# One scale per batch for the queries of the last two batches of a block-sparse attention with a rational feed-forward

## The chip, the cores and the metric

The kernel runs on one core of a Trainium2 chip. The time is that of the device in microseconds, the median of three runs. The core has five instruction streams that run side by side, each in order: PE (TensorE, the matmuls), DVE (VectorE), ACT (ScalarE), POOL (GpSimd), and SP (SyncE), which here issues the DMA transfers. They wait for each other by semaphores.

## The reference

Four batches (B = 4) of 8 heads, 768 positions and 64 features go through a block-sparse attention (blocks of 32; each block sees its neighbours, the first and the last block, and three sampled ones), and the 3072 x 512 result goes through a feed-forward whose middle is a quotient of polynomials:

```python
scores = scale * np.matmul(q, k.transpose(0, 1, 3, 2))
...
attn = np.exp(scores)
attn = attn / (np.sum(attn, axis=-1, keepdims=True) + 1e-09)
return np.matmul(attn, v).astype(np.float32)
...
h = x @ w_in
P = a[0] + a[1] * h + a[2] * h2 + a[3] * h3
Q = 1.0 + np.abs(b[0]) * np.abs(h) + np.abs(b[1]) * h2
g = P / (Q + 1e-06)
return (g @ w_out).astype(np.float32)
```

## The kernel before

The program first makes a list of pieces of work (`Op`: engine, price, what must be done before, which buffers it takes, a due number `prio`), and `issue` then puts them in one fixed order per engine, by a model of the prices. A change of a few pieces therefore moves others too. At run time every engine works through its list in order and waits where a list says so.

Queries and keys are split into two float16 parts, high and low, after they were multiplied by a power of two. That scale comes from a bound on the largest entry: ACT sums absolute values (`bound`, L392), PE turns the 128 sums onto one partition's row (L343, a 128 x 128 transpose), DVE takes their maximum (L348) and makes the scale in four small instructions (L351 to L360).

For keys and values there is one such scale a batch (`prep`): six loads `ld` of 128 x 512 (L588), six bounds, one scale, and for keys a second round of loads (L540) that are split, turned on PE (L668) and stored. All of these loads, and the staging of the output, take buffers of one ring (`r_ld`, three, and four more once the weights are decoded).

For queries there is one scale for each tile of four blocks (`prep_q`, six tiles a batch, 24 in all): SP loads `ldq` (L711), ACT bounds it (L392), PE turns the sums (L343), DVE makes the scale and the factor of the scores `cq` (L729 to L735), POOL makes the high part (L154), DVE the low part (L386), PE turns both (L741), ACT takes them from PSUM (L745), and SP swaps halves (L749). `ldq` has one buffer, which is free again after the low part.

Around it run the attention of one block after the other (scores L884, maxima L894 and L923 on DVE, exponentials L912 on ACT, transposes L953, values L1010, and for four blocks together the normalisation L1044 and the transposes L1056) and the feed-forward in units: 24 matmuls `into` (L1121 to L1123), squares and the like on ACT (L1128 to L1152), the quotient on DVE (L1135 to L1166, ending with the high part `gh`, L1156, and the low part `gl`, L1166), and 12 matmuls `out` (L1177 with `gh`, L1178 with `gh`, L1179 with `gl`, four times).

In what follows the batches are called first to fourth (b = 0 to 3 in the code), and the query tiles of a batch first to sixth.

Of the kernel before, what the change touches and what calls it, by code (L numbers as in the profile page):

```python
# [23 lines left out]
def kernel(  # L24
# [117 lines left out]
    def among(key, home, **prices):  # L142

        d = {{"ve": VE, "sc": SC, "po": PO}[n]: p for n, p in prices.items()}
        return {home: d[home], **(d if key in ALT else {})}
# [395 lines left out]
                          in_=src[b, g * HU:(g + 1) * HU, t * CH:(t + 1) * CH].rearrange("h (p s) d -> p h (s d)", s=2))  # L541

    PLAIN = B
    s_kall = [Slot(r_kg) for _ in kgs]

    def prep(b, when):
# [7 lines left out]
        before = {}  # L554
        if first:
            rings = [[(r_tt, "tt", p2), (r_ab, "ab", p2), (r_sq, "sq", p2)], [(r_pr, "pr", p3), (r_ld, "ld", p3)]]
        for w in range(2):
            mx, lds, los = {}, {}, []

            def mx_tile(mx=mx):  # L560
                if 0 not in mx:
                    mx[0] = p4.tile([P, 8], F32, name="mx")
                return mx[0]

            for j in range(n):
                def one(j, w=w, lds=lds, mx_tile=mx_tile):
# [11 lines left out]
                    def load():  # L578
                        if first:
                            nb = {"tt": 3, "pr": 4}.get(tag)  # L580
                            d["ld"] = pool.tile([P, 512], F32, name=tag, bufs=nb)
                            if w:
                                nc.sync.dma_start(out=d["ld"], in_=v[b].rearrange("h (a r) d -> (h a) (r d)", a=P // H)[:, j * 512:(j + 1) * 512])
                            else:
                                load_unit(k, b, *units[j], d["ld"])
                        else:
                            d["ld"] = new_ld(slot)
                            nc.sync.dma_start(out=d["ld"], in_=(k, v)[w][b].rearrange("h (a r) d -> (h a) (r d)", a=P // H)[:, j * 512:(j + 1) * 512])  # L588

                    def most():  # L590
                        bound(d["ld"], mx_tile()[:, j:j + 1])
# [6 lines left out]
            def out_scale(s, inv):  # L598
                kv[b][4] = p4.tile([P, 1], F32, name="xscale", bufs=B)
                nc.vector.tensor_copy(out=kv[b][4], in_=s)  # L600

            def largest(mx=mx, w=w):
                nc.vector.tensor_reduce(out=mx[0][:, 6:7], in_=mx[0][:, 0:n], axis=AX.X, op=ALU.max)
# [94 lines left out]
    def prep_q(b, t, prio, before):  # L698
# [1 line left out]


        d = qt[b, t] = {}
        s_ld, s_hl, s_sc, s_ps = Slot(r_ldq), Slot(r_hlq), Slot(r_scq), Slot(r_sp)
        d["slot"], d["cslot"] = Slot(r_qa), Slot(r_cq)

        def load():
            d["ld"] = p1.tile([P, 512], F32, name="ldq")
# [16 lines left out]
            split16(d["ld"], sc[0], d["hl"], 0, None)  # L724

        def factor():
            d["cc"] = p4.tile([P, 2], F32, name="cq")
            d["c"], d["cn"] = d["cc"][:, 0:1], d["cc"][:, 1:2]
            nc.vector.scalar_tensor_tensor(out=d["c"], in0=sc[1], scalar=SCALE, in1=kv[b][2], op0=ALU.mult, op1=ALU.mult)  # L729

# [20 lines left out]
            d["q"] = [x.rearrange("p (h g) r -> p g h r", g=2) for x in (qa, qc)]  # L751

        o_ld = Op(SY, [(650, 262144 // 2 // len(runs(t)))] * 2 * len(runs(t)), load, (), prio - 1, takes=[s_ld], behind=before)
        o = Op(SC, 613, most, [o_ld], prio, uses=[s_ld])
        o, sc = scales(lambda: d["mx"][:, 0:1], "scq", [o], prio, [s_sc])
        h = Op(among("q", PO, po=671, ve=396, sc=613), 0, high, [o], prio, takes=[s_hl], uses=[s_ld, s_sc])
        l = Op(VE, 663, low, [h], prio, uses=[s_ld, s_hl, s_sc])
        d["oc"] = row(VE, [(70, factor), (69, factor2), (69, factor3)], [o, k_scale[b]], prio, takes=[d["cslot"]], uses=[s_sc])
        x = Op(TE, 445, transposes, [l], prio, takes=[s_ps], uses=[s_hl])
        x = Op(SC, 904, evac, [x], prio, takes=[d["slot"]], uses=[s_ps])  # L760
        d["oq"] = Op(SY, [(650, 131072)] * 2, swap, [x], prio, uses=[d["slot"]])
# [42 lines left out]
    def attention(b, j, prio):  # L804
# [15 lines left out]
        for m, x in enumerate(xs):  # L820
            def one(m, x):
# [84 lines left out]
                def exps():  # L906
                    st = d["st"]
                    for g in range(2):
                        if "sm" not in G:
                            G["sm"] = p4.tile([P, 3, 2 * XB], F32, name="sm", bufs=2)  # L910
                        total = G["sm"][:, 0, 2 * e4 + g:2 * e4 + g + 1]
                        nc.scalar.activation(out=prs[x][:, g], in_=prs[x][:, g], func=AF.Exp, scale=Q["c"], bias=st[:, 6 + g:7 + g],  # L912
                                             accum_out=total if n == 1 else st[:, 8 + 2 * m + g:9 + 2 * m + g])

                return s_pr, exps
# [4 lines left out]
            return 71, lambda: nc.vector.tensor_tensor(out=d["st"][:, 0:2], in0=d["st"][:, 0:2], in1=d["st"][:, 2 * e:2 * e + 2], op=ALU.max)  # L920

        def negative():
            nc.vector.tensor_scalar(out=d["st"][:, 6:8], in0=d["st"][:, 0:2], scalar1=Q["cn"], scalar2=PS_EXP * math.log(2.0), op0=ALU.mult, op1=ALU.add)  # L923

        omax = row(VE, [larger(e) for e in range(1, n)] + [(130, negative)], omax, prio[-1], uses=[s_st, Q["cslot"]])
        for m, x in enumerate(xs):
            s_pr, exps = d[m]
            oexp.append(Op(SC, 1172, exps, [omax], prio[m] + 0.1, takes=[G["s_sm"]] if e4 == 0 and m == 0 else [],
                           uses=[s_pr, s_st, Q["cslot"]] + ([] if e4 == 0 and m == 0 else [G["s_sm"]])))

        def total(e):
            def run():
# [324 lines left out]
    def when(b):  # L1257
        if b == 0:
            return lambda w, stage, j: (-83.96, -78.19)[w] + stage * 0.5
        p0 = part_prio(first_of[b])  # L1260
        A = [8.9, 8.52] if b == 1 else [11.69, 8.81]
        return lambda w, stage, j: p0 - A[stage] + (w * 6 + j) * (([0.5, 0.5] if b == 1 else [0.85, 0.83])[stage])

    prep(0, when(0))
    chain["edges"] = Op(PO, 1400, edges, [o for t in range(NCH) for o in k_evac[0, t]], -40, uses=s_kall)
# [61 lines left out]
```

## Time and profile before

| | |
|---|---|
| median of three runs | 891.03 us (888.12 to 893.66) |
| the profiled execution | 892.74 us, of it 890.9 us from the first to the last instruction |
| PE busy with matmuls | 833.8 us, 94% |
| DVE, ACT, POOL busy | 737.1 us (83%), 676.7 us (76%), 109.9 us (12%) |
| mean granted TensorE clock | 0.973 of full speed |
| chain that ended last | 65% PE, 9% DMA, 9% DVE, 7% ACT, 6% SP's issuing |
| moved by DMA | 148.01 MB, 166 GB/s |

Busy time counts instructions of the engine itself, not waits. The first 290 us hold the decoding of the weights and much waiting; after that PE has a matmul in flight nearly all the time.

### The profile page before, as it was taken

The page shows a single profiled execution, that of the slowest core. Times are in us where ns is not written, and L with a number is a line of the kernel's source. Part 1 is how long each engine was busy: PE and PEld are TensorE (multiplying, and loading weights), DVE is VectorE, ACT ScalarE, POOL GpSimd, SP SyncE. Part 2 cuts the span into 40 slices and gives each one's busy share as a digit, 9 for nine tenths or more (in the row PEclk, how much of TensorE's full clock was granted, in tenths as well). Part 3 has the DMA queues.
Part 4 walks back from the last instruction along what each step waited for, and adds up shares of the span by engine and source line. Part 5 has one row for each costly group of instructions (what it writes and reads, how often), then busy time and mean ns, then how long its engine had stood idle before and what let it go on. Part 6 is the DMA issues. An engine that isn't in the chain of part 4 may idle for free.

```text
span 890.9 us, 27280 instructions
## 1 busy us (share of the span) xinstructions
PE 833.8 (94%) x10349; PEld 646.3 (73%) x10349; DVE 737.1 (83%) x1826; ACT 676.7 (76%) x1451; POOL 109.9 (12%) x114
## 2 busy tenths in 40 slices
PE   8988686897899999899999999999999999999997
PEld 4454464675678787688877787778888777788885
DVE  5657998899999888689877978779888887788885
ACT  6777897897687878598767887898768678767563
POOL 1113631616310000100000000100000000000000
PEclk9999798798999999899999999999999999999999
DMA  7798589778856965699756965698567566640000
GB/s 201 186 169 197 169 180 207 209 199 226 177 152 160 261 184 150 149 230 230 160 147 168 277 176 148 166 235 223 152 152 179 153 172 157 165 108 24 1 24 24
DMA packets 238481, 148.01 MB, mean 166 GB/s; under 512 B 16016, under 2 KB 222736, under 8 KB 238352
## 3 DMA queue, kind: packets, MB, share of 16 engines
q1 hardware_dynamic: 238352, 146.29, 65.6%
q8 instruction: 82, 1.34, 0.7%
q14 instruction: 47, 0.39, 0.2%
HBM read 128.92 MB, written 11.01 MB: 157 GB/s over the span
## 4 chain that ended last, share of the span: by engine, by line
PE 65%; DMA 9%; DVE 9%; ACT 7%; SPq 6%; issue 3%; ACTq 0%; POOL 0%; DVEq 0%; POOLq 0%
PE acc L1177 9%; PE acc L1178 8%; PE acc L1179 8%; PE ph L1121 8%; PE ph L1122 7%; PE ph L1123 7%; PE av L1010 5%; PE sp L884 4%; PE pt L953 4%; DMA vg<-in_v_dram 3%; DMA ldq<-in_q_dram 2%; ACT pr L912 1%; ACT scrap L392 1%; DMA wl<-in_moe_w_out_dram 1%; SPq L980 1%
## 5 line engine op out<-in xcount | busy, mean ns | idle before, releaser
L1121 PE MATMUL ph<-xh,wi 128*128 128x256 f16 x768 | 213.1, 278 | 0.0
L1122 PE MATMUL ph<-xl,wi 128*128 128x256 f16 x768 | 211.9, 276 | 0.0
L1123 PE MATMUL ph<-xh,wi 128*128 128x256 f16 x768 | 211.7, 276 | 0.0
L912 ACT ACTIVATE pr<-pr,st,cq 128x256 f32<-128x256 f32 x224 | 132.2, 593 | 46.4 <-DVE st L923 46.2
L1177 PE MATMUL acc<-wo_h,gh 128*128 128x512 f32 x384 | 165.4, 431 | 0.2 <-ACT ld L150 0.2
L1179 PE MATMUL acc<-wo_h,gl 128*128 128x512 f32 x384 | 154.5, 402 | 3.5 <-DVE gl L1166 3.5
L1178 PE MATMUL acc<-wo_l,gh 128*128 128x512 f32 x384 | 153.9, 401 | 0.8 <-POOL wo_l L459 0.8
L1145 DVE SCALAR_TENSOR_TENSOR ab<-sq,absb,ab 128x512 f32<-128x512 f32 x96 | 73.7, 768 | 46.4 <-ACT ab L1142 46.3
L1128 ACT ACTIVATE sq<-ph,fc 128x512 f32<-128x512 f32 x96 | 65.5, 682 | 57.3 <-PE ph L1123 56.9
L1121 PEld LDWEIGHTS <-wi 128*128 128x128 f16 x768 | 76.2, 99 | 28.7 <-issue 15.8
L894 DVE CUSTOM_DVE_ANT_1 pr<-sp,bias 128x256 f32<-128x256 f32 x224 | 84.7, 417 | 9.4 <-PE sp L884 9.3
L1179 PEld LDWEIGHTS acc<-wo_h,gl 128*128 128x128 f32 x384 | 73.5, 191 | 22.4 <-DVE gl L1166 4.8
L1177 PEld LDWEIGHTS acc<-wo_h,gh 128*128 128x128 f32 x384 | 74.0, 193 | 17.0 <-issue 2.3
L1156 DVE SCALAR_TENSOR_TENSOR gh<-tt,par,rr 128x512 fp32r<-128x512 f32 x96 | 72.7, 757 | 14.0 <-PE acc L1178 13.4
L1178 PEld LDWEIGHTS acc<-wo_l,gh 128*128 128x128 f32 x384 | 73.9, 193 | 13.5 <-POOL wo_l L459 1.7
L154 POOL TENSOR_SCALAR hlq<-ldq,scq 128x512 f16<-128x512 f32 x24 | 21.4, 892 | 504.9 <-DVE scq L360 306.6
L1123 PEld LDWEIGHTS <-wi 128*128 128x128 f16 x768 | 76.1, 99 | 9.6
L953 PE MATMUL pt<-ident,pr 128*128 128x128 f32 x448 | 76.8, 293 | 6.1 <-ACT pT L150 4.6
L1010 PE MATMUL av<-vg,pT 128*32 128x64 f32 x3584 | 74.2, 224 | 8.8 <-DMA vg<-in_v_dram 4.8
L1122 PEld LDWEIGHTS <-wi 128*128 128x128 f16 x768 | 76.2, 99 | 8.0
L953 PEld LDWEIGHTS pt<-ident,pr 128*128 128x128 f32 x448 | 68.0, 206 | 18.3 <-ACT pT L150 6.2
L1010 PEld LDWEIGHTS av<-vg,pT 128*32 128x32 f32 x3584 | 56.4, 111 | 33.9 <-issue 10.9
(144 smaller groups left out, 1651.5 us busy)
## 6 DMA issues: line engine op xcount, KB each, us to landing
vg<-in_v_dram SPq DMA_DIRECT2D x312, 64.0 KB, 3.3
vg<-in_v_dram SPq DMA_DIRECT2D x88, 192.0 KB, 3.9
vg<-in_v_dram SPq DMA_DIRECT2D x24, 512.0 KB, 5.4
kall<-ks SPq DMA_DIRECT2D x49, 192.0 KB, 3.7
kall<-ks SPq DMA_DIRECT2D x147, 64.0 KB, 2.1
ld<-in_k_dram SPq DMA_DIRECT2D x36, 256.0 KB, 5.6
wl<-in_moe_w_in_dram SPq DMA_DIRECT2D x32, 256.0 KB, 4.8
wl<-in_moe_w_out_dram SPq DMA_DIRECT2D x16, 512.0 KB, 4.6
```

The source lines that it names most:

```text
L894: nc.vector.tensor_tensor_reduce(out=prs[x][:, g].rearrange("p (s r) -> p s r", r=BLK), in0=h["sp"][:, g].rearrange("p (s r) -> p s r", r= ...
L912: nc.scalar.activation(out=prs[x][:, g], in_=prs[x][:, g], func=AF.Exp, scale=Q["c"], bias=st[:, 6 + g:7 + g], accum_out=total if n == 1 e ...
L953: nc.tensor.transpose(pp[:, jj * P:(jj + 1) * P], cols, ident)
L1010: nc.tensor.matmul(av[rows, g], pT[:, 2 * g + kt, rows] if plain else pT[:, 2 * g + kt, pa_, rows], vf[:, g * HG + h4, kt * D:(kt + 1) * D ...
L1121: nc.tensor.matmul(o, wh, xh[:, :, cc], start=(cc == 0), stop=False)
L1122: nc.tensor.matmul(o, wh, xl[:, :, cc], start=False, stop=False)
L1123: nc.tensor.matmul(o, wl, xh[:, :, cc], start=False, stop=(cc == NCC - 1))
L1145: nc.vector.scalar_tensor_tensor(out=d["ab"], in0=d["sq"], scalar=absb[:, 1:2], in1=d["ab"], op0=ALU.mult, op1=ALU.add)
L1156: nc.vector.scalar_tensor_tensor(out=d["gh"], in0=d["tt"], scalar=par[:, 0:1], in1=d["rr"], op0=ALU.add, op1=ALU.mult)
L1177: nc.tensor.matmul(acc[:, t], ghs, wo_h[:, f], start=(new and e == 0), stop=False)
L1178: nc.tensor.matmul(acc[:, t], ghs, wo_l[:, f], start=False, stop=False)
L1179: nc.tensor.matmul(acc[:, t], gls, wo_h[:, f], start=False, stop=(last and e == 1))
```

## The change

For the third and the fourth batch (`QB = 2`) `prep` runs a pass more, `w == 2`, ahead of those of keys and values: six loads `ld` of the whole batch of queries, six bounds on ACT, one maximum on DVE, one transpose on PE and one scale. The six tiles of such a batch have no bound, transpose and scale of their own any more: the high part waits for the load `ldq` and for the batch's scale alone. Their factor `cq` is made once a batch. The first two batches are as before.

```diff
+    QB = 2
+    q_scale = {}
...
-        for w in range(2):
+        for w in ([2] if b >= QB else []) + [0, 1]:
...
-                            nc.sync.dma_start(out=d["ld"], in_=(k, v)[w][b].rearrange("h (a r) d -> (h a) (r d)", a=P // H)[:, j * 512:(j + 1) * 512])
+                            nc.sync.dma_start(out=d["ld"], in_=(k, v, q)[w][b].rearrange("h (a r) d -> (h a) (r d)", a=P // H)[:, j * 512:(j + 1) * 512])
...
+            if w == 2:
+                def largest(mx=mx):
+                    nc.vector.tensor_reduce(out=mx[0][:, 6:7], in_=mx[0][:, 0:n], axis=AX.X, op=ALU.max)
+
+                o = Op(VE, 75, largest, los, when(w, 0, n - 1))
+                q_scale[b] = scales(lambda mx=mx: mx[0][:, 6:7], "scqb", [o], when(w, 0, n - 1))
+                continue
...
-        o = Op(SC, 613, most, [o_ld], prio, uses=[s_ld])
-        o, sc = scales(lambda: d["mx"][:, 0:1], "scq", [o], prio, [s_sc])
-        h = Op(among("q", PO, po=671, ve=396, sc=613), 0, high, [o], prio, takes=[s_hl], uses=[s_ld, s_sc])
-        l = Op(VE, 663, low, [h], prio, uses=[s_ld, s_hl, s_sc])
-        d["oc"] = row(VE, [(70, factor), (69, factor2), (69, factor3)], [o, k_scale[b]], prio, takes=[d["cslot"]], uses=[s_sc])
+        if own:
+            o = Op(SC, 613, most, [o_ld], prio, uses=[s_ld])
+            o, sc = scales(lambda: d["mx"][:, 0:1], "scq", [o], prio, sl_sc)
+        else:
+            o, sc = q_scale[b]
+        h = Op(among("q", PO, po=671, ve=396, sc=613), 0, high, [o, o_ld], prio, takes=[s_hl], uses=[s_ld] + sl_sc)
+        l = Op(VE, 663, low, [h], prio, uses=[s_ld, s_hl] + sl_sc)
+        if own or t == 0:
+            d["oc"] = row(VE, [(70, factor), (69, factor2), (69, factor3)], [o, k_scale[b]], prio, takes=d["cslot"], uses=sl_sc)
+            d["first"] = d
+        else:
+            d["first"], d["oc"] = qt[b, 0], qt[b, 0]["oc"]
...
-        return lambda w, stage, j: p0 - A[stage] + (w * 6 + j) * (([0.5, 0.5] if b == 1 else [0.85, 0.83])[stage])
+        return lambda w, stage, j: p0 - A[stage] + ((w * 6 if w < 2 else -3) + j) * (([0.5, 0.5] if b == 1 else [0.85, 0.83])[stage])
```

In the changed kernel PE, DVE, ACT and POOL keep their order up to the place of 290 us in the trace of before; PE's list is the same up to 342.7 us and again from 797.5 us on. Line numbers behind the first edit are higher by 2 to 19 (L1166 is L1185, L923 is L942, L711 is L723, L588 is L590). Three places of the new order matter here, all at the sixth query tile of the third batch.

DVE, where the quotient of a unit ends with `gl`. Before:

```order
L1162 SCALAR_TENSOR_TENSOR tt<-tt,par,ab 128x512
L1044 TENSOR_TENSOR xn<-av,sm 128x512
L1166 TENSOR_TENSOR gl<-tt,rr 128x512
L348 TENSOR_REDUCE scq<-sp 128x1
L351 TENSOR_SCALAR scq<-scq 128x1
```

Now:

```order
L1181 SCALAR_TENSOR_TENSOR tt<-tt,par,ab 128x512
L1063 TENSOR_TENSOR xn<-av,sm 128x512
L386 SCALAR_TENSOR_TENSOR hlq<-ldq,scqb,hlq 128x8x64
L942 TENSOR_SCALAR st<-st,cqb 128x2
L1185 TENSOR_TENSOR gl<-tt,rr 128x512
```

The low part of the query tile (L386) has moved up by eight places and now stands ahead of `gl`; the negative maxima (L923, now L942), which stood ahead of L1162, stand behind it too.

SP, the loads ahead of that tile's `ldq` (the ISA rows prepare an address that was read at run time). Before:

```order
L856 DMA kall<-ks 128x256
L711 DMA ldq<-in_q_dram 64x4x128 x2
L974 DMA vg_111<-in_v_dram 48x8x128
L980 ISA
L980 DMA vg_111<-in_v_dram 16x8x128
```

Now:

```order
L875 DMA kall<-ks 128x256
L590 DMA ld<-in_k_dram 128x512
L723 DMA ldq<-in_q_dram 64x4x128 x2
L993 DMA vg_111<-in_v_dram 48x8x128
L999 ISA
```

A load of keys of the fourth batch, the fifth of six for its bound, stands just ahead of `ldq`; the fourth of them stands ten DMAs further up, ahead of a group `vg`, and the sixth behind the next group `kall`. In the trace of before all six were issued between 484.3 and 497.0 us, ahead of the fifth query tile's load.

PE, behind the 24 matmuls `into` of the same unit. Before:

```order
L343 MATMUL sp<-ident,mxq 128x128
L1177 MATMUL acc<-wo_h,gh 128x512
L1178 MATMUL acc<-wo_l,gh 128x512
L1179 MATMUL acc<-wo_h,gl 128x512
```

Now:

```order
L1075 MATMUL sp<-ident,xn 128x128 x4
L1196 MATMUL acc<-wo_h,gh 128x512
L1197 MATMUL acc<-wo_l,gh 128x512
L1198 MATMUL acc<-wo_h,gl 128x512
```

The transpose of the tile's own bound is gone, the four transposes L1056 (now L1075) have taken its place, and the `out` matmuls follow at once; the transposes of the tile itself (L741, now L753) follow the twelve `out` matmuls.

## Rows read from the trace of the kernel before

**Rows 1.** The page, section 1: busy us (share of the span) and instructions.
```profile
PE 833.8 (94%) x10349; PEld 646.3 (73%) x10349; DVE 737.1 (83%) x1826; ACT 676.7 (76%) x1451; POOL 109.9 (12%) x114
```

**Rows 2.** Busy times by stretch: length, engines, granted clock, DMA share, GB/s.
```profile
550.00:575.00 25.00, 22.77 (x253) 18.29 (x251) 19.32 (x47) 17.34 (x33) 3.60 (x4) 0.93 0.62 164
600.00:625.00 25.00, 25.00 (x342) 20.72 (x338) 23.12 (x71) 21.86 (x49) 0.69 (x1) 1.00 0.83 226
```

**Rows 3.** Waits of the whole run: total us, times, longest us.
```profile
ACT scrap L392 <- DMA ldq<-in_q_dram: 20.4, 8, 5.9
```

**Rows 4.** PE's timeline, sixth query tile, second batch: start, length, what, idle before.
```profile
359.10 0.27 PE L1123 MATMUL ph<-xh,wi 128*128 128x256 f16 x1
362.73 0.48 PE L343 MATMUL sp<-ident,mxq 128*128 128x128 f32 x1 [3.36 <-ACT scrap L392]
...
369.45 0.27 PE L1121 MATMUL ph<-xh,wi 128*128 128x256 f16 x1
```

**Rows 5.** PE's timeline at the sixth query tile of the third batch.
```profile
556.60 0.27 PE L1123 MATMUL ph<-xh,wi 128*128 128x256 f16 x1
559.10 0.32 PE L343 MATMUL sp<-ident,mxq 128*128 128x128 f32 x1 [2.23 <-ACT scrap L392]
...
564.54 0.27 PE L343 MATMUL sp<-ident,mx 128*128 128x128 f32 x1
564.65 0.27 PE L1121 MATMUL ph<-xh,wi 128*128 128x256 f16 x1
```

**Rows 6.** PE's timeline: the same matmuls without a wait, first and next after.
```profile
493.01 0.48 PE L1177 MATMUL acc<-wo_h,gh 128*128 128x512 f32 x1
...
496.88 0.29 PE L884 MATMUL sp<-kall,qa 128*32 128x256 f16 x4
```

**Rows 7.** PE's timeline: the other idle times of the last two batches.
```profile
487.70 1.09 PE L953 MATMUL pt<-ident,pr 128*128 128x128 f32 x4 [0.29 <-ACT pr L912]
...
491.19 0.65 PE L1010 MATMUL av<-vg,pT 128*32 128x64 f32 x32 [0.43 <-ACT pT L150]
...
741.26 0.65 PE L1010 MATMUL av<-vg,pT 128*32 128x64 f32 x32 [0.69 <-ACT pT L150]
```

**Rows 8.** ACT's timeline: bounds that waited for `ldq`, and one place later used.
```profile
486.34 0.63 ACT L392 ACTIVATE scrap<-ldq 128x512 f16<-128x512 f32 x1 [4.04 <-DMA ldq<-in_q_dram]
...
546.19 0.62 ACT L1152 ACTIVATE rr<-rr 128x512 f32<-128x512 f32 x1
...
558.33 0.63 ACT L392 ACTIVATE scrap<-ldq 128x512 f16<-128x512 f32 x1 [4.79 <-DMA ldq<-in_q_dram]
...
734.89 0.63 ACT L392 ACTIVATE scrap<-ldq 128x512 f16<-128x512 f32 x1 [1.82 <-DMA ldq<-in_q_dram]
```

**Rows 9.** DVE's timeline around the same tile.
```profile
554.86 0.22 DVE L923 TENSOR_SCALAR st<-st,cq 128x2 f32<-128x2 f32 x1
...
555.65 0.68 DVE L1044 TENSOR_TENSOR xn<-av,sm 128x512 f32<-128x512 f32 x1
556.25 0.68 DVE L1166 TENSOR_TENSOR gl<-tt,rr 128x512 fp32r<-128x512 f32 x1
...
562.07 0.75 DVE L386 SCALAR_TENSOR_TENSOR hlq<-ldq,scq,hlq 128x512 f16<-128x512 f32 x1
```

**Rows 10.** POOL's timeline: the high part of the same tile.
```profile
560.57 0.69 POOL L154 TENSOR_SCALAR hlq<-ldq,scq 128x512 f16<-128x512 f32 x1 [25.77 <-DVE scq L360]
```

**Rows 11.** The chain that ended last, in order of time: start, us, what.
```profile
549.88 0.45 SPq L851
...
553.30 0.68 SPq L711
...
554.03 4.22 DMA ldq<-in_q_dram
```

**Rows 12.** SP's timeline: issuing, start and length.
```profile
489.66 1.37 SPq L588 DMA_DIRECT2D ld<-in_k_dram  x3
...
545.96 1.36 SPq L974 DMA_DIRECT2D vg<-in_v_dram  x1
...
559.32 1.39 SPq L856 DMA_DIRECT2D kall<-ks  x3
```

**Rows 13.** DMA issues by kind: count, KB each, median us to landing.
```profile
ld<-in_k_dram SPq DMA_DIRECT2D x36, 256.0 KB, 5.6
```

More of the change, by code (lines that the diff above doesn't have):

```diff
@@ L561, in mx_tile @@
                 if 0 not in mx:
-                    mx[0] = p4.tile([P, 8], F32, name="mx")
+                    mx[0] = p4.tile([P, 8], F32, name="mx", bufs=5)
                 return mx[0]
@@ L702, in prep_q @@
         d = qt[b, t] = {}
-        s_ld, s_hl, s_sc, s_ps = Slot(r_ldq), Slot(r_hlq), Slot(r_scq), Slot(r_sp)
-        d["slot"], d["cslot"] = Slot(r_qa), Slot(r_cq)
+        s_ld, s_hl, s_ps = Slot(r_ldq), Slot(r_hlq), Slot(r_sp)
+        own = b < QB
+        sl_sc = [Slot(r_scq)] if own else []
+        d["slot"], d["cslot"] = Slot(r_qa), [Slot(r_cq)] if b < QB else []
         def load():
@@ L726, in factor @@
         def factor():
-            d["cc"] = p4.tile([P, 2], F32, name="cq")
+            d["cc"] = p4.tile([P, 2], F32, name="cq" if own else "cqb")
             d["c"], d["cn"] = d["cc"][:, 0:1], d["cc"][:, 1:2]
@@ L911, in exps @@
                         total = G["sm"][:, 0, 2 * e4 + g:2 * e4 + g + 1]
-                        nc.scalar.activation(out=prs[x][:, g], in_=prs[x][:, g], func=AF.Exp, scale=Q["c"], bias=st[:, 6 + g:7 + g],
+                        nc.scalar.activation(out=prs[x][:, g], in_=prs[x][:, g], func=AF.Exp, scale=Q["first"]["c"], bias=st[:, 6 + g:7 + g],
                                              accum_out=total if n == 1 else st[:, 8 + 2 * m + g:9 + 2 * m + g])
@@ L922, in negative @@
         def negative():
-            nc.vector.tensor_scalar(out=d["st"][:, 6:8], in0=d["st"][:, 0:2], scalar1=Q["cn"], scalar2=PS_EXP * math.log(2.0), op0=ALU.mult, op1=ALU.add)
-        omax = row(VE, [larger(e) for e in range(1, n)] + [(130, negative)], omax, prio[-1], uses=[s_st, Q["cslot"]])
+            nc.vector.tensor_scalar(out=d["st"][:, 6:8], in0=d["st"][:, 0:2], scalar1=Q["first"]["cn"], scalar2=PS_EXP * math.log(2.0), op0=ALU.mult, op1=ALU.add)
+        omax = row(VE, [larger(e) for e in range(1, n)] + [(130, negative)], omax, prio[-1], uses=[s_st] + Q["cslot"])
         for m, x in enumerate(xs):
@@ L928, in attention @@
             oexp.append(Op(SC, 1172, exps, [omax], prio[m] + 0.1, takes=[G["s_sm"]] if e4 == 0 and m == 0 else [],
-                           uses=[s_pr, s_st, Q["cslot"]] + ([] if e4 == 0 and m == 0 else [G["s_sm"]])))
+                           uses=[s_pr, s_st] + Q["cslot"] + ([] if e4 == 0 and m == 0 else [G["s_sm"]])))
         def total(e):
```

## The prediction

> **What bounds the kernel now.** I read the busy times on the page of the profile first, then stretches of 25 us, then the waits, then PE's timeline at its gaps. PE is busy 94% of the span, DVE 83%, ACT 76%, POOL 12% [rows 1]. In the second half a plain stretch has a matmul in flight for all of its 25.00 us at full clock, while DVE and ACT keep idle time [rows 2]. So from some 290 us on only two things shorten the run: matmuls that go away, and gaps on PE that close. DVE's instructions are free as long as PE does not wait for them. Of the gaps, the large ones end in the same way: ACT waits for the load `ldq` of a query tile, eight times, 20.4 us together [rows 3], and PE stands at the tile's transpose of the bound, L343, until ACT is through: 3.36 us at the sixth tile of the second batch [rows 4], 2.23 us at the sixth tile of the third [rows 5]. Besides these there are three gaps of 0.29, 0.43 and 0.69 us in the last two batches [rows 7].
>
> A gap costs more than itself. Behind the gap of 3.36 us the next 22 matmuls (twelve `out`, eight transposes, two L343) took 369.45 - 362.73 = 6.72 us [rows 4], behind the one of 2.23 us 564.65 - 559.10 = 5.55 us [rows 5]; the twelve and eight took 496.88 - 493.01 = 3.87 us without a gap [rows 6], with two L343 at 564.65 - 564.54 = 0.11 us each [rows 5] 4.09 us. The granted clock was 0.93 in the stretch around the second gap, 1.00 in the plain one [rows 2]. That is 2.6 us more behind the long gap, 1.5 us behind the short one; the places cost 6.0 and 3.7 us in all.
>
> **The change, part by part.**
>
> *Transposes removed.* Twelve L343 go, two come. In a stream each takes 0.11 us of PE [rows 5]: -1.1 us. PE is full there, so all of it counts. The Trainium skill (Perfetto Trace Analysis, Identifying the Most-Contended Engine) would have TensorE's headroom read from the busy share of its weight loads and not of its matmuls; that share is 20.72 of 25 us in the plain stretch [rows 2], which leaves 17%, and by that rule alone this term would be nothing and the sum 1.1 us higher. I go by the timeline, where the next matmul follows L343 at once.
>
> *Small DVE instructions.* 79 rows fewer on DVE, at most 0.22 us each (the length of L923 [rows 9]), so up to 17 us. DVE is not the bound: nothing. If a DVE chain did hold PE, it would be worth up to these 17 us; no gap of [rows 4, 5, 7] ends at one.
>
> *Bounds.* ACT loses twelve bounds at the tiles and gets twelve in the two passes: nothing in sum, but ACT no longer waits for `ldq` in the last two batches. Such waits were 4.04, 4.79 and 1.82 us [rows 8]. Behind the first PE had the gaps of 0.29 and 0.43, behind the last that of 0.69 [rows 7]: they close, -1.4 us. The middle one is the gap of 2.23 us, below.
>
> *The second batch's sixth tile* keeps its own bound. In the new order the four transposes L1056 stand ahead of the waiting L343, where they run in the gap: 20 matmuls of [rows 6] are 0.19 us each, four are 0.8 us at the most. They are of the short kind, I take -0.5 us (bounds 0 and -0.8).
>
> *The third batch's sixth tile: the wait moves to DVE.* The low part (L386) now stands on DVE ahead of `gl` (L1166), which the third `out` matmul needs. DVE ended the normalisation at 555.65 + 0.68 = 556.33 and went straight on to `gl` [rows 9]; now it waits there for the load. The second half of `ldq` was issued at 554.03 and landed 4.22 us later, at 558.25, at the end of a chain of SP's own issuing [rows 11]. Two loads of keys now stand ahead of it since 545.96; one costs SP 1.37 / 3 = 0.46 us [rows 12], so it lands at about 559.2. From there: 0.69 us on POOL [rows 10], 0.1 us for each of two hand-overs (ACT began 0.08 us after the landing [rows 8, 11]), then L386, L923 and `gl`, 0.75 + 0.22 + 0.68 us [rows 9]: `gl` is ready at 561.7. PE ends `into` at 556.60 + 0.11 = 556.7 [rows 5], has four transposes and two `out` matmuls, 6 x 0.19 = 1.2 us [rows 6], and stands from 557.9 on: a gap of 3.8 us for one of 2.23. Behind it I take the 2.6 us of the nearest gap, 3.36 us [rows 4]. 6.4 for 3.7 us: +2.7 us. Bounds: -3.7 if DVE finds the tile ready, +4.1 if the landing takes the 5.6 us that is the median of loads of 256 KB [rows 13].
>
> *The new passes.* Twelve loads of 256 KB more, through the same ring as the loads of keys. The third batch's six take the places that the keys' had, and the keys' second round moves from there to where its parts are made, some 10 us ahead of need; nothing. In the fourth batch the keys' six loads for the bound are strung out, since the ring is full. The fourth is issued just ahead of 545.96 [rows 12], lands 4.22 to 5.6 us later [rows 11, 13], and ACT reaches its bound at 546.19 + 0.62 = 546.8 [rows 8]: ACT waits 3 us or more, with the next evacuation L150 behind it, for which PE's values wait. Waits of ACT without an L343 behind them cost PE 0.7 us each [rows 7, 8]: +0.7 us. The fifth load meets the same tile's wait, where PE stands anyway. Bounds for this place 0 and 6.0 us, as at the dearest gap [rows 4].
>
> *Sum:* -1.1 - 1.4 - 0.5 + 2.7 + 0.7 = **+0.4 us**. Against the profiled execution (892.74 us, 890.9 of it the span) that is 893.1; this execution lay 1.7 us above the median of 891.03, so on the median **891.4 us**.
>
> **Rivals.**
>
> *1. The waits simply vanish.* The scale is there long before, only POOL waits for the load, and POOL is 12% busy [rows 1]. Then -1.1 - 1.4 - 0.5 - 3.7 = -6.7 us: **884.3**. For it: at the other eleven tiles the low part stands late enough on DVE. Against it: at this one it does not, by 3 us. It holds if `ldq` lands before about 555.4 (556.33 less POOL's 0.69 and two hand-overs), or if the execution has PE later there than SP. The Trainium skill (Perfetto Trace Analysis, Optimization Strategy) says to look for what releases the gaps of the engine to be filled and to make that start sooner; that is this case and gives 884.3. The rows bear out its first half: the gaps do end at the bound. Should the second batch's gap go too, another 5.5 us fall away (878.8); nothing in the order says so.
>
> *2. The fourth batch's own scales become the wait.* The sixth load of keys now stands behind SP's group at 559.32 + 1.39 = 560.7 [rows 12]. Its bound, maximum and transpose L343 on PE follow, some 1.2 us (0.63 on ACT [rows 8], the rest an estimate from DVE's and PE's small rows); PE's place for that L343 is 24 `into` matmuls behind 564.65, at 0.11 us: 567.3 at the earliest [rows 5]. It decides whether the load takes more than 5.4 us; the median is 5.6 [rows 13]. Against it: PE and ACT come there later for other work too. Price 6.0 us as in [rows 4]: **897.4**. The batch's query scale has the same form some 25 us earlier (loads 5 and 6 just before their bounds); both together give **903.4**.
>
> *3. The change only renames the waits.* Twelve bounds for twelve; loads of keys wait on ACT where loads of queries did, and gaps close and open alike: **891.0**.
>
> **How the numbers follow.** Forecast 0.50, rival 1 0.25 (of it 0.06 with the second batch's gap), rival 2 0.17 (0.09 of it with both waits), rival 3 0.08. The likeliest gives 891.4, its own range is 888 to 895. For 8 in 10 the range takes in rival 1 and the single wait of rival 2: 884 to 898. What a measurement of this kernel can tell from no change is about 1%, so 882.1 to 899.9 is the same: faster 0.06, slower 0.09, same 0.85.
>
> **What the changed profile would show.** For the sum: at the third batch's sixth tile DVE idle 3 us or more ahead of L386, released by POOL or `ldq`, PE idle ahead of the `out` matmul with `gl`, released by DVE, and a clock under 1.00 there; no gap on PE near the places of 487, 491 and 741 us; the gap of the second batch's tile still there. ACT waiting for `ld` near 547 and 553. The forecast is wrong if that DVE wait is missing or under 1 us (rival 1), if an L343 of the sums of a whole batch has a gap of over 1 us ahead of it (rival 2), or if PE gaps of over 1 us appear behind transfers that are not named here.

## The result, and the profile after

The changed kernel takes 883.70 us (median of 16 runs, 879.36 to 890.18), the kernel before 890.21 us on the same chips. The ratio is 0.9932, with a 95% interval of 0.9913 to 0.9951: 6.0 us less, 4.4 to 7.7. Forecast were 891.4 us and a range of 884 to 898; it came out at the time of the first rival (884.3), though not, as the experiments show, for all of that rival's reasons. The profiled execution took 885.49 us, 883.7 of it the span, at a mean granted clock of 0.985 (before 0.973).

The page, section 1 (busy us, share of the span, instructions), answers to [rows 1]:

```profile
PE 825.0 (93%) x10339; PEld 642.5 (73%) x10339; DVE 732.0 (83%) x1748; ACT 677.0 (77%) x1448; POOL 112.8 (13%) x117
```

ACT's waits for a load ahead of a bound, from 340 to 800 us (total us, times, longest us); the second line answers to [rows 3]:

```profile
ACT scrap L392 <- DMA ld<-in_v_dram: 8.5, 6, 2.0
ACT scrap L392 <- DMA ldq<-in_q_dram: 4.5, 1, 4.5
ACT scrap L392 <- DMA ld<-in_k_dram: 3.6, 3, 1.4
ACT scrap L392 <- DMA ld<-in_q_dram: 0.7, 1, 0.7
```

The same stretch in the kernel before:

```profile
ACT scrap L392 <- DMA ldq<-in_q_dram: 16.9, 5, 5.9
ACT scrap L392 <- DMA ld<-in_v_dram: 0.4, 1, 0.4
```

Both sums are 17.3 us. The waits have been renamed, as rival 3 had it, but they have also been cut up: five of 3.4 us on the average for `ldq` before, now eleven of 1.6. The sums are those of this pair of profiles: in a second profile of each kernel (e9 and e1 below) they are 17.6 us before, in five waits, and 11.0 us after, in nine.

PE's own gaps after (start, length, what, idle time before):

```profile
358.68 0.32 PE L343 MATMUL sp<-ident,mxq 128*128 128x128 f32 x1 [1.52 <-ACT scrap L392]
...
382.62 0.29 PE L903 MATMUL sp<-kall,qa 128*32 128x256 f16 x4 [2.35 <-ACT kt L150]
...
390.76 0.39 PE L972 MATMUL pt<-ident,pr 128*128 128x128 f32 x1 [1.23 <-ACT pT L150]
...
569.60 0.27 PE L678 MATMUL sp<-ident,hl 128*128 128x128 f16 x2 [1.61 <-ACT kt L150]
...
576.38 0.26 PE L1029 MATMUL av<-vg,pT 128*32 128x64 f32 x3 [1.10 <-ACT pT L150]
```

The first answers to [rows 4]. Nothing answers to [rows 5] or [rows 7]: those gaps are gone. Four gaps are new beside this profile of the kernel before, all in the two stretches where the next batch's keys and values are bounded and split; a second profile of the kernel before (e9) has gaps in these stretches too. How the last arises is seen on ACT, where a bound of values waits and the evacuation that PE needs stands behind it:

```profile
575.12 0.63 ACT L392 ACTIVATE scrap<-ld 128x512 f16<-128x512 f32 x1 [1.46 <-DMA ld<-in_v_dram]
...
575.75 0.58 ACT L150 ACTIVATE pT<-pt 128x512 f32<-128x512 f32 x1
```

By stretch (length, PE busy, granted clock, DMA share, GB/s), before, in the profile that the prediction rests on:

```profile
340.00:375.00 35.00, 31.64 (x388) 0.90 0.61 157
375.00:410.00 35.00, 35.00 (x461) 1.00 0.99 232
540.00:562.00 22.00, 19.77 (x244) 0.95 0.56 157
562.00:612.00 50.00, 49.76 (x678) 0.99 0.87 220
700.00:770.00 70.00, 69.31 (x915) 1.00 0.65 165
```

and after:

```profile
340.00:375.00 35.00, 33.48 (x444) 1.00 0.76 180
375.00:410.00 35.00, 31.41 (x417) 1.00 0.93 226
540.00:562.00 22.00, 22.00 (x289) 1.00 0.76 201
562.00:612.00 50.00, 47.21 (x615) 1.00 0.92 228
700.00:770.00 70.00, 70.00 (x944) 1.00 0.65 168
```

In these five PE idles longer than before, 7.90 us for 6.51, but at full clock throughout: 0.10 x 35 + 0.05 x 22 + 0.01 x 50 = 5.1 us of lost clock are gone. With the ten transposes (1.1 us) that makes -5.1 - 1.1 + 1.4 = -4.8 us. The two spans differ by 7.2; another 2.6 us of it arose ahead of the first `out` matmul of the 25th unit (at 351.09 us before and 348.47 after), where the two orders are the same but for the last 8 us. They are chance: in e9, the program of before again, that matmul starts at 347.14 us. In this pair of profiles the idle time has moved from the query tiles (340 to 375 and 540 to 562 us) into the stretches of keys (375 to 410 and 562 to 612 us).

The second pair reads otherwise. The same five stretches summed, in e9 (before) and then in e1 (changed):

```profile
sum 212.00, PE 200.56; mean PE 40.11
sum 212.00, PE 207.59; mean PE 41.52
```

PE is idle 11.44 us before, with 1.7 us of lost clock, and 4.41 us after, with none. Idle time and lost clock together (a little too much, since a fall can begin inside a gap) go from 11.6 and 13.1 us in the two profiles before to 7.9 and 4.4 us in the two after. That is of the size of the gain in both pairs; whether it comes as clock or as idle time differs from one execution to the next.

### The profile page after: what moved, and what is told of

The parts are those of the page before. It is cut to its first block, busy times and chain, and to the rows that moved or that the text cites. A ratio compares the mean times of both kernels' runs of the same rounds, so it can differ in the third digit from the quotient of the medians.

```text
span 883.7 us, 27171 instructions
## 1 busy us (share of the span) xinstructions
PE 825.0 (93%) x10339; PEld 642.5 (73%) x10339; DVE 732.0 (83%) x1748; ACT 677.0 (77%) x1448; POOL 112.8 (13%) x117
## 4 chain that ended last, share of the span: by engine, by line
PE 61%; DVE 11%; DMA 9%; SPq 7%; ACT 6%; issue 3%; POOL 1%; ACTq 0%; DVEq 0%
PE ph L1140 8%; PE acc L1196 8%; PE acc L1198 7%; PE acc L1197 7%; PE ph L1142 7%; PE ph L1141 7%; PE av L1029 5%; PE sp L903 4%; PE pt L972 4%; DMA vg<-in_v_dram 2%; DMA wl<-in_moe_w_out_dram 2%; SPq L999 2%; ACT pr L931 1%; ACT scrap L392 1%; DMA qc<-qa 1%
## 5 line engine op out<-in xcount | busy, mean ns | idle before, releaser
L1196 PE MATMUL acc<-wo_h,gh 128*128 128x512 f32 x384 | 163.6, 426 | 0.2 <-ACT ld L150 0.2
L931 ACT ACTIVATE pr<-pr,st,cqb 128x256 f32<-128x256 f32 x112 | 66.1, 593 | 32.7 <-DVE st L942 32.7
L1196 PEld LDWEIGHTS acc<-wo_h,gh 128*128 128x128 f32 x384 | 72.9, 190 | 17.6 <-issue 2.3
L150 ACT ACTIVATE pT<-pt 128x512 f32<-128x512 f32 x112 | 66.2, 591 | 13.3 <-PE pt L972 12.5
```

Source lines behind the costliest of these rows:

```text
L1196: nc.tensor.matmul(acc[:, t], ghs, wo_h[:, f], start=(new and e == 0), stop=False)
```

## The experiments

All ratios are to the kernel before on the same chip, with 95% intervals. The planner writes the five lists anew at every edit, so other work moves too; only e1, e7, e9 and e10 keep the order of their parent.

| run | what | median us | ratio |
|---|---|---|---|
| e1 | changed kernel again | 883.27 | 0.9936 (0.9913 to 0.9960) |
| e2 | pass, third batch alone | 889.35 | 1.0004 (0.9984 to 1.0025) |
| e3 | pass, fourth batch alone | 886.45 | 0.9962 (0.9948 to 0.9976) |
| e4 | passes made, not used | 885.65 | 0.9965 (0.9943 to 0.9988) |
| e5 | constant scale, no pass | 884.97 | 0.9953 (0.9927 to 0.9980) |
| e6 | before, `ldq` sooner | 889.19 | 1.0003 (0.9984 to 1.0022) |
| e7 | changed, one `ldq` later | 885.34 | 0.9967 (0.9946 to 0.9989) |
| e8 | before, one `ldq` sooner | 888.38 | 0.9988 (0.9968 to 1.0008) |
| e9 | before again | 888.42 | 0.9992 (0.9969 to 1.0016) |
| e10 | changed, half the bytes of bounds | 882.20 | 0.9925 (0.9901 to 0.9950) |
| e11 | changed, keys loaded once | 881.71 | 0.9914 (0.9887 to 0.9940) |
| e12 | before, keys loaded once | 884.50 | 0.9950 (0.9931 to 0.9970) |
| e13 | constant scale, fourth batch | 886.94 | 0.9969 (0.9946 to 0.9992) |
| e14 | before, keys and values later | 894.71 | 1.0058 (1.0032 to 1.0084) |
| e15 | changed, passes earlier | 881.48 | 0.9904 (0.9874 to 0.9934) |
| e16 | e11, pass for second batch too | 880.56 | 0.9887 (0.9859 to 0.9915) |
| e17 | e15 and e16 together | 893.08 | 1.0037 (1.0020 to 1.0054) |
| e18 | e6 and e12 together | 886.73 | 0.9970 (0.9953 to 0.9987) |

**Which part gains (e1 to e5, e13).** e1 has no edit.

> The changed kernel once more, unedited, for a second profile. Theory A (the gain lies in PE's gaps at the query tiles, and part of it is given back by new gaps where the keys of the next batch are prepared): about 883.7 us; the gaps of PE near 383, 391, 570 and 576 us (2.35, 1.23, 1.61, 1.10 us in the first profile) come again, and none is at the third batch's sixth tile. Rival B (the gaps fall where chance puts them in one execution): the gaps stand at other places or are under half as long. The lead of 2.6 us that the changed kernel had at its 25th unit (348.47 for 351.09 us), ahead of nearly all that differs, should be gone or of another size if it is chance.

The gain came again (0.9936). Three of the gaps came too, at 357.7, 380.9 and 570.5 us (1.73, 1.64, 0.50 us; the last answers to that of 576 us above), those of 391 and 570 us did not, and one of 1.62 us stood at 697.7. The first `out` matmul of the 25th unit came at 346.8 us, so the lead there is chance.

```diff
-        for w in ([2] if b >= QB else []) + [0, 1]:
+        for w in ([2] if b == 2 else []) + [0, 1]:
...
-        own = b < QB
+        own = b != 2
...
```

> The pass for the third batch alone; the fourth batch's tiles keep their own scales. Theory A, from the starts of the units in the two profiles: the second batch's gap -4.7 us, the third batch's tiles -5.2, the keys of the third batch prepared later +3.6: 890.2 - 6.3 = 884 us. Rival C (each tile that loses its bound, transpose and small DVE instructions gives the same, wherever it stands): half of the 6.5 us, 887 us. Gaps near 383 and 391 us are there by theory A, none near 570 and 576.

```diff
-    QB = 2
+    QB = 3
```

> The pass for the fourth batch alone; the third batch's tiles keep their own scales. Theory A: the fourth batch's tiles -1.7 us (the gap of 0.69 and six transposes), its keys prepared later +3.1: 890.2 + 1.4 = 891.6 us, and the gap of some 2.2 us at the third batch's sixth tile stands. Rival C: 887 us.

```diff
-        own = b < QB
+        own = True
...
```

> Both passes are made (loads, bounds, one scale each), and the tiles still make and use their own scales as before: the passes' cost alone. Theory A: +3.6 and +3.1 us for the keys prepared later, and the gaps at the query tiles stay: 890.2 + 6.7 = 897 us, with no gain. Rival C: two more transposes and twelve more bounds where ACT has idle time, 0.2 us: 890.4 us. Rival D (what gains is the new order around the second batch's sixth tile, which the pass brings by itself): 886 us.

All three went against theory A: the third batch gives nothing in total (-1.4 to +2.2 us), the fourth 3.4 us, and the passes, which should only cost, 3.1 us. Rival C has the fourth batch (887 us) and not the third. Rival D has the time of e4 (886 us) and not its reason: e2 has PE's order of the changed kernel up to 535.5 us, the second batch's sixth tile included, and gains nothing. What goes with the gain of e4 can be seen in the order. At the third batch's sixth tile the passes push the bound's transpose on PE back: the second half of `ldq` is issued at 546.19 us and PE comes to L343 at 553.98, 7.8 us later, where before it came 559.10 - 2.23 - 554.03 = 2.8 us later [rows 5, 11]. Neither ACT nor PE waits there any more, though the bound is still made (ACT, then PE):

```profile
550.34 0.61 ACT L392 ACTIVATE scrap<-ldq 128x512 f16<-128x512 f32 x1
```

```profile
553.98 0.27 PE L343 MATMUL sp<-ident,mxq 128*128 128x128 f32 x1
```

That this is what gains is not shown: e6 below closes the same gap and gains nothing, and in e4 the wait for `ldq` at the fourth batch's sixth tile is gone as well, with PE's gap near 741 us; another wait, of 4.19 us at 703.99, costs PE 0.39 us.

```diff
-        for w in ([2] if b >= QB else []) + [0, 1]:
+        for w in range(2):
...
-            o, sc = q_scale[b]
+            o, sc = fixed()
```

Here `fixed` sets 2^12 and 2^-12 once for all these tiles.

> No pass; the tiles of the third and fourth batch take a constant scale (2 to the 12th), so what is left out is the bound on their queries, and nothing is loaded for it. Theory E (half of the gain is the missing bounds of the tiles, half is the new order at the second batch's sixth tile, which only the third batch's pass brings): the gap of 3.3 us there stands and behind it the clock falls, the gaps at the later tiles go, none opens near 381 and 570 us: 886 us. Theory A, that the passes only cost: the gain of 6 us and the 3 to 6 us given back, 878 us. Rival D (the order alone gains): 889 us, as before.

Without passes 4.2 us are gained, near theory E (886 us), far from A and D. As E had it, the second batch's gap stands (3.72 us); against it, one of 1.89 us opens at 580 us. e13 is the same for the fourth batch alone (`QB = 3`).

> No pass; the fourth batch's tiles alone take a constant scale (the bound on their queries is left out). The two profiles of the kernel before have PE idle 0.7 and 2.9 us at that batch's sixth tile, the second with 1.5 us of low clock behind it. Theory K (the missing bounds of the fourth batch's tiles are the gain, whatever pass is made): 2.5 to 4 us less than before, 885 to 886.5 us, as the pass for that batch alone gave (0.9962). Rival L (what gains is how the pass displaces the preparation of the keys): 888.5 to 889 us.

2.8 us (0.7 to 4.8), next to the 3.4 of e3. That is nearer to theory K than to rival L, though the interval, 885.4 to 889.4 us by the ratio, takes in all of rival L. But for the one constant made at the start, every engine's order in e13 is that of before up to some 600 us (PE's up to 602.0, and again from 797.5). So what it gains lies with the fourth batch's tiles, which make no scale of their own, and needs no pass.

**What one profile is worth (e9).** No edit.

> The kernel before once more, unedited, for a second profile. If the first profile is typical, the gaps of 3.36 and 2.23 us at the sixth tiles of the second and third batch come again with the low clock behind them; the start of the 25th unit (351.09 us there, 346.4 to 348.5 in the programs that were the same up to that place) shows how much of the lead of the others is chance.

PE's gaps in this second profile of the kernel before:

```profile
357.40 0.32 PE L343 MATMUL sp<-ident,mxq 128*128 128x128 f32 x1 [1.97 <-ACT scrap L392]
...
381.23 0.26 PE L1010 MATMUL av<-vg,pT 128*32 128x64 f32 x4 [1.66 <-ACT pT L150]
...
552.96 0.32 PE L343 MATMUL sp<-ident,mxq 128*128 128x128 f32 x1 [1.92 <-ACT scrap L392]
...
576.88 0.26 PE L1010 MATMUL av<-vg,pT 128*32 128x64 f32 x3 [1.75 <-ACT pT L150]
...
732.94 0.39 PE L953 MATMUL pt<-ident,pr 128*128 128x128 f32 x1 [0.84 <-ACT pr L912]
...
737.96 0.26 PE L1010 MATMUL av<-vg,pT 128*32 128x64 f32 x4 [1.95 <-ACT pT L150]
```

The same program, and another picture. The gap at the second batch's sixth tile is 1.97 us for 3.36, and gaps in the stretches of keys (381, 577 us) are there without any change. The place at 741 us that [rows 7] show with 0.69 us costs 2.79 here, and the clock falls behind it (last but two: granted clock):

```profile
735.00:740.00 5.00, 3.05 (x52) 0.93 0.68 207
740.00:745.00 5.00, 5.00 (x50) 0.73 0.43 121
```

That is 0.35 + 1.35 us more, 4.5 us in all where 0.7 was priced. ACT's wait for `ldq` that goes with it was 4.55 us for 1.82 [rows 8].

**The step of the forecast, forced (e7).**

```diff
-            for g in range(2):
+            for g in (0, 1) * (2 if (b, t) == (2, 5) else 1):
```

> The changed kernel, with the load ldq of the third batch's sixth tile issued twice into the same buffer: the tile is there some 4 us later, and the order on the other engines is the same. By the prediction's step (the low part stands ahead of gl on DVE) DVE then waits 3.5 to 4.5 us ahead of the low part, PE stands about 3 us for gl and its clock falls: 883.5 + 5 = 888.5 us. If DVE's wait is covered by other work of PE: 883.5 to 884.5 us.

DVE in e7, at the third batch's sixth tile, and POOL:

```profile
547.83 0.69 DVE L1063 TENSOR_TENSOR xn<-av,sm 128x512 f32<-128x512 f32 x1 [0.39 <-PE av L1029]
552.40 0.75 DVE L386 SCALAR_TENSOR_TENSOR hlq<-ldq,scqb,hlq 128x512 f16<-128x512 f32 x1 [3.87 <-POOL hlq L154]
553.06 0.22 DVE L942 TENSOR_SCALAR st<-st,cqb 128x2 f32<-128x2 f32 x1
553.19 0.69 DVE L1185 TENSOR_TENSOR gl<-tt,rr 128x512 fp32r<-128x512 f32 x1
```

PE in e7:

```profile
549.92 0.39 PE L1198 MATMUL acc<-wo_h,gl 128*128 128x512 f32 x1
...
553.21 0.62 PE L753 MATMUL sp<-ident,hlq 128*128 128x128 f16 x8 [0.79 <-DVE hlq L386]
554.07 0.50 PE L972 MATMUL pt<-ident,pr 128*128 128x128 f32 x2 [0.24 <-ACT pr L931]
```

and by stretch:

```profile
550.00:555.00 5.00, 3.88 (x23) 1.00 0.80 176
555.00:560.00 5.00, 4.59 (x77) 1.00 0.99 260
```

The DVE wait is just the forecast's: 3.87 us, by its numbers 3.8. Its price is not. The `out` matmul with `gl` ran at 549.92 us, over three microseconds ahead of the `gl` at 553.19, and so cannot read it. PE stood at the tile's own transposes (0.79), then 0.24 and 0.41 us (557.53), with the clock at 1.00. The medians are 885.34 us here and 883.3 to 883.7 without the delay; the intervals of the two overlap, so 2 us is the size, not a sure figure. The 888.5 us of the forecast's step lie above the interval (883.7 to 887.5 us by the ratio); the other expectation, 883.5 to 884.5, is at its lower end.

**Loads sooner (e6, e8).** In the kernel before:

```diff
-        ... load, (), prio - 1, takes=[s_ld], behind=before)
+        ... load, (), prio - 1 - (1.0 if b > 1 else 0), takes=[s_ld], behind=before)
```

> The kernel before, with nothing changed but that the loads ldq of the third and fourth batch are due one unit (some 7.5 us) sooner; every tile keeps its bound. If the late load is what holds PE at the bounds of these tiles, the gaps near 487, 491, 559 and 741 us close: 889 - 1.4 - 3.7 = 884 us. If the bound, transpose and small DVE instructions themselves cost, nothing is gained: 889 us. The second batch's gap stands in either case.

At the third batch's sixth tile the wait for `ldq` and the gap are gone from the trace, but the total is that of before. PE begins the `into` matmuls behind it at 557.9 us, for 564.65 [rows 5], some 3.6 us of it won at the tile. In the stretch that follows it stood for a key tile, with the clock at 0.97 from 562 to 612 us, and at the fourth batch's sixth tile, where ACT still waited 2.06 us for `ldq`, the gap stayed:

```profile
576.41 0.29 PE L884 MATMUL sp<-kall,qa 128*32 128x256 f16 x4 [2.26 <-ACT kt L150]
...
737.89 0.32 PE L1010 MATMUL av<-vg,pT 128*32 128x64 f32 x8 [0.94 <-ACT pT L150]
```

So the edit closed one of the two places. Whether the stretch of keys takes back what was won there, the profiles don't settle: from 562 to 612 us PE is idle 2.26 us here and 2.22 in e2, where the third batch's gap is closed, but also 2.48 and 2.54 in e3 and e13, where 1.51 and 0.61 us of it stand, and 1.87 in e9.

e8 does it for the second batch's sixth tile alone, by 0.5 (`(b, t) == (1, 5)`).

> The kernel before, with the load ldq of the second batch's sixth tile alone due half a unit sooner. Theory E: the gap of 3.3 us at that tile's bound and the low clock behind it (20 matmuls in 6.7 for 3.9 us) go, and nothing else changes: 889 - 6 = 883 us, as much as the whole change gives. If such a gap is made up for later (PE is not what ends last): 888 to 889 us.

There the gap at L343 is 0.00, one of 1.24 us opens behind it (355.5 us, for a group `vg`), five smaller ones stand between 380 and 393 us (0.42 to 0.88), and 1.1 us are gained for 6, with an interval that takes in no gain at all. From 375 to 410 us PE is idle 2.85 us, and in e9, with the tile's gap in place, 2.80. Theory E fell with this and with e9.

**What holds PE in the stretches of keys (e10 to e12, e14, e15).** e10, in the loads for bounds of the last two batches:

```diff
-  nc.sync.dma_start(out=d["ld"], in_=...[:, j * 512:(j + 1) * 512])
+  m = 256 if b >= 2 else 512
+  nc.sync.dma_start(out=d["ld"][:, :m], in_=...[:, j * 512:j * 512 + m])
...
```

> The changed kernel with half the bytes in the loads for the bounds of the third and fourth batch (18 loads a batch, 128 KB less each; ACT reads the half it has twice, so its time and every order are the same; the bounds thus leave out half the entries). Theory F (from some 375 to 410 and 570 to 612 us the DMA engines, whose share is 1.0 there, set when PE comes out, and a gap closed ahead of them is given back): 2.36 MB less in each stretch, up to 9 us of their time, so the gaps near 381 and 570 us and the give-back behind them (1.5 to 3.6 and 0.9 to 3.2 us) go: 878 to 881 us. Rival G (what holds PE there is SP's order and its waits, or ACT in line, and not bytes): 883.5 us.

Half the bytes gave about 1 us, within the uncertainty, and gaps of 1.15, 0.69 and 1.44 us stayed: bytes alone are not what decides. Rival G is nearer, though the interval (880.3 to 884.6 us by the ratio) reaches down to theory F.

e11 and e12:

```diff
+    KEEP = 2
...
-                    if first and w == 0:
+                    if (first or b >= KEEP) and w == 0:
                         slot.left += 2
...
+                            if b >= KEEP and w == 0:
+                                return load_unit(k, b, *units[j], d["ld"])
...
-        if first:
+        if first or b >= KEEP:
             s_ld = d["slot"]
```

> The changed kernel, where the keys of the third and fourth batch are loaded once: the six loads for the bound stay in their buffers until they are split, as the first batch has it, and the second round falls away (1.57 MB a batch, nothing left out of the result). Theory F: 2 to 5 us less, 879 to 881.5 us. Rival H (six of seven buffers of the ring held, so the loads of values and the staging of the output come late): 886 us or more. Rival G: 883.5 us.

> The same saving of loads in the kernel before, with no pass. Theory F: before, PE comes to these stretches late enough, 888 us as before, since only what is ahead of them and the low clock hold it; at most 1 us less. If the loads cost wherever they are: 884 us.

Some 2 us off the changed kernel, within the uncertainty and the least that theory F had, but 4.4 off the kernel before, where it had none: the second round of six loads a batch costs there too. Theory F, that bytes decide and only for a PE that comes early, falls.

e14:

```diff
-  p0 - A[stage] + (w * 6 + j) * ...
+  p0 - A[stage] + (w * 6 + j + (2 if b > 1 else 0)) * ...
```

> The kernel before, with the preparation of keys and values of the third and fourth batch due two places (1.7 units) later and no pass. Rival L: the later keys leave the third and fourth batch's query loads undisturbed, 885 to 886 us, as the passes alone gave (0.9965). Theory K: later keys only make PE wait more where they are used (the gaps near 381 and 577 us grow): 890 to 893 us.

e15:

```diff
-  ((w * 6 if w < 2 else -3) + j)
+  ((w * 6 if w < 2 else -6) + j)
```

> The changed kernel, with its passes due three places (2.55 units) earlier, so that the loads of keys are displaced less. If the displaced keys cost (PE idle of 1.6 to 3.6 and 0.7 to 2.8 us in the two stretches of keys): 881 to 882 us. Rival L, that their being displaced is part of the gain: 885 to 886.5 us.

These two end rival L. Keys and values later cost 5 us; passes made sooner, so that the keys are displaced less, give some 2 us more than the change, where rival L had less gain (the intervals of e15 and the change overlap). In e15 ACT's waits ahead of bounds from 340 to 800 us are 7.6 us, for 17.3 and 11.0 in the two profiles of the change, and PE is idle 0.09 us in the second stretch of keys, for 2.79 and 0.69:

```profile
375.00:410.00 35.00, 33.17 (x466) 1.00 1.00 243
562.00:612.00 50.00, 49.91 (x634) 1.00 0.98 244
```

**Better versions (e16 to e18).** e16 is e11 with `QB = 1`; e17 is that with the `-6` of e15; e18 joins the edits of e6 and e12.

> The pass for the second batch too, and the keys of the third and fourth batch loaded once. If the second batch's sixth tile, whose bound holds PE 1.5 to 3.7 us in all profiles that have it early, gives what it costs: 881.7 - 1.7 - 0.6 = 879.5 us. If the stretch of keys behind it takes that back (as in the kernel before, where 4.1 us gained by 373 us were 0.6 at 400 us): 881 to 882 us.

> Three steps together: the pass for the second batch too, all passes due three places earlier, the keys of the third and fourth batch loaded once. If their gains add: 883.5 less 2.0 (earlier passes), less 3 (the other two) = 878.5 us. If they are the same gain, the stretches of keys relieved once: 880.5 us.

> The kernel before with both edits that were tried apart: the loads ldq of the third and fourth batch due one unit sooner (1.0003 alone) and the keys of these batches loaded once (0.995 alone). Theory M (closing the third batch's gap gives 4 us, which the stretch of the fourth batch's keys takes back; with less work in that stretch it stays): 884.5 - 3 = 881.5 us or less. If closing the gap gives nothing in itself: 884.5 us, as with the keys alone.

e16, at 880.56 us, between its two expectations, is the fastest by its median, clear of the kernel before; its interval and that of the changed kernel (0.9913 to 0.9951) just overlap, and e11 and e15 lie within it. The steps don't add: e17 is slower than before by 3.3 us, and PE is idle 2.4 us already between 285 and 340 us and 2.3 us between 410 and 540. What in its order does that was not tried. e18 lies between e6 and e12: theory M, that the early loads' gain would stay once the stretch of keys is relieved, fell.

## Why the prediction was wrong

**The step that failed** is "the third batch's sixth tile: the wait moves to DVE", +2.7 us. Two things in it were wrong.

*Who needs `gl`.* It said that `gl` behind the low part is what "the third `out` matmul needs", and let PE stand for it at once. With the numbers left in the names the order of the changed kernel says otherwise (first DVE, then PE):

```text
L1185 TENSOR_TENSOR gl_9737<-tt_9470,rr_9479 128x512
...
L386 SCALAR_TENSOR_TENSOR hlq_9866<-ldq_9772,scqb_6173,hlq_9866 128x8x64
L942 TENSOR_SCALAR st_9815<-st_9815,cqb_6826 128x2
L1185 TENSOR_TENSOR gl_9895<-tt_9611,rr_9639 128x512
```

```text
L1198 MATMUL acc_9760<-wo_h_105,gl_9737
...
L753 MATMUL sp_9924<-ident16_96,hlq_9866 128x128
...
L1198 MATMUL acc_9760<-wo_h_105,gl_9895
```

The `out` of this place reads the `gl` made a unit earlier; the one behind the low part is needed at the next `out`, some 8 us on. Names without numbers hid it. e7 prices the step: a DVE wait of 3.87 us costs PE 1.4 us of idle time and no clock, where 6.4 us stood in the sum.

*When the load lands.* After the change, on DVE, POOL, PE and SP:

```profile
550.58 0.69 DVE L1063 TENSOR_TENSOR xn<-av,sm 128x512 f32<-128x512 f32 x1
551.72 0.75 DVE L386 SCALAR_TENSOR_TENSOR hlq<-ldq,scqb,hlq 128x512 f16<-128x512 f32 x1 [0.45 <-POOL hlq L154]
...
552.52 0.68 DVE L1185 TENSOR_TENSOR gl<-tt,rr 128x512 fp32r<-128x512 f32 x1
```

```profile
550.99 0.70 POOL L154 TENSOR_SCALAR hlq<-ldq,scqb 128x512 f16<-128x512 f32 x1 [42.38 <-DMA ldq<-in_q_dram]
```

```profile
551.75 0.48 PE L1196 MATMUL acc<-wo_h,gh 128*128 128x512 f32 x1
...
552.29 0.39 PE L1198 MATMUL acc<-wo_h,gl 128*128 128x512 f32 x1
```

```profile
546.48 0.42 SPq L590 DMA_DIRECT2D ld<-in_k_dram  x1
547.00 1.37 SPq L723 DMA_DIRECT2D ldq<-in_q_dram  x2
```

DVE waits 0.45 us. POOL starts 0.40 us ahead of the end of `into` (551.28 + 0.11); the forecast had the landing at 559.2 for an `into` that ends at 556.7, 2.5 us behind it. About 1 us of the difference of 2.9 is the transfer (3.2 us from 547.7, where its second half is issued, for 4.22 [rows 11]). The rest is SP: it issues that half 3.7 us ahead of the end of `into`, where before it was 2.7, and the forecast had counted 0.9 us of delay for the two loads of keys. One thing that left SP's list was not counted, the swap of the fifth tile, for which SP had stood 2.7 us at 538.08 us before and which now comes at 525.9; that it is the cause was not tried.

**Rival 1** gave the time, and its condition held but for DVE's wait of 0.45 us. Its parts did not: 3.7 us for the third batch's tile and 0.7 for the fourth's, where e2 and e3 measure nothing and 3.4 us. The third's gap does close (540 to 562 us above), and it does in e2 and e6, but the time doesn't fall there. A stretch of keys follows the third batch's tile and none the fourth's, where the gain stays (e3, e13); that this is the reason is not shown. That rival 1's sum meets the time is thus in part luck. The Trainium skill (Perfetto Trace Analysis, Optimization Strategy) says to make what releases the gaps start sooner. e6 did that at the third batch's tile: the gap closed, and the time stayed at 1.0003 (0.9984 to 1.0022), so there the advice gave nothing that can be measured.

**Rival 2** fell: no L343 of a whole batch's sums has a gap ahead of it. **Rival 3**, that the waits are only renamed, is right for ACT in the first pair of profiles (17.3 us for 17.3) and not in the second (17.6 and 11.0), and its time, 891.0 us, is wrong.

**Smaller terms.** The gaps at 487 and 491 us (-0.7) are not in e9 either, and stand with 1.11 and 0.43 us in e3, where PE's order up to 513.7 us is that of before: they come and go with the execution. The wait for the fourth batch's keys (+0.7) came on ACT (1.42 us at 542.16) and cost PE nothing. "Nothing" for the third batch's displaced keys was too little: 1.6 to 3.6 us of idle time from 375 to 410 us in the two profiles, of which e9 shows up to 2.8 to be there anyway. The -1.1 us of ten transposes was not measured alone.

**What was priced from one execution** was the second fault. The range rested on gaps of 0.69, 2.23 and 3.36 us, which a second profile shows as 2.79, 1.92 and 1.97. By the runs with one batch this fault is the larger in time. In the forecast's own terms, the second batch's -0.5 apart, the third batch is -0.55 (five transposes) - 0.7 (487 and 491 us) + 2.7 = +1.45 us and the fourth -0.55 - 0.7 (741 us) + 0.7 (its keys) = -0.55 us; measured are +0.4 (-1.4 to +2.2, e2) and -3.4 (-4.6 to -2.1, e3). So the third batch's total came out within the uncertainty though its mechanism was wrong, and the mis-sized term is the gap near 741 us, 0.7 us in the sum and 4.5 in e9.

**What stays open.** e2 and e3 together would give 0.9966, the change gives 0.9932 and 0.9936, and the passes unused 0.9965. Whether the missing 3 us are the order that both passes make together, or the uncertainty of some 2 us in each, these runs don't tell.

## What to carry to other kernels

Before a wait is priced on the engine it moves to, follow the names with their numbers to the instruction that reads the delayed result: software pipelining can put it a unit away. A gap that closes need not shorten the run: e2, e6 and e8 each closed one and gained nothing clear of the uncertainty, while the gain that came twice (e3, e13) lies with the last batch's tiles. So force each gap by itself and measure the whole. And take a second profile of the kernel before, before a gap of 1 to 4 us goes into a sum: here the same place cost 0.7 us in one execution and 4.5 in the next.

## What was not expected of the hardware

The clock did not follow the idle time by its sum, nor by the length of one gap. The rows show it at full speed or at half of it. It stood at half from 362 to 368 us, behind the gap of 3.36 us [rows 4] (length, PE busy, granted clock, DMA share, GB/s):

```profile
362.00:368.00 6.00, 5.27 (x15) 0.50 0.79 164
```

It stood at half too from 560 to 563 us, behind that of 2.23 us [rows 5], and fell behind 0.84 and 1.95 us close together (e9). Behind single gaps of 1.52 to 2.35 us after the change, and of 1.92 and 1.97 us in e9, the stretches show 1.00. From 285 us on, in all profiles, the five gaps of over 3 us (the first profile of before, e3, e5, e13, e16) each went with a fall that took 3.4 us of clock. Those of 1.5 to 2.6 us lie on both sides: 2.60 in e14 and 1.95 in e16 lost 1.7 us, while this one in e8 lost none (1.00 from 553.6 to 558.6 us):

```profile
553.56 0.32 PE L343 MATMUL sp<-ident,mxq 128*128 128x128 f32 x1 [2.59 <-ACT scrap L392]
```

So the price of 1.5 us that the forecast took for the short gap was that of one execution: e9 has 1.92 us at the same place, and no fall.
